# A fused gated recurrence and capacity-limited mixture of experts: where the zero rows are written, how wide, and what keeps TensorE busy around the selection

## The chip, the cores and the metric

The kernel runs on one core of one Trainium2 chip. The metric is device time in microseconds of one execution. Before the change the median of three runs is 306.29 us (305.9 to 307.69).

## The reference

`x`, `r_gate` and `i_gate` have the shape (4, 5056, 256). The first stage is a linear recurrence over time, the second a mixture of 8 experts over its N = 20224 output rows, in which each expert takes at most `capacity` = 80 tokens:

```python
a_t = exp(8 * sigmoid(r_gate) * log(clip(sigmoid(a_param), 1e-6, 1 - 1e-6)))
x_gated = sqrt(max(1 - a_t * a_t, 1e-6)) * sigmoid(i_gate) * x
h = a_t[:, t] * h + x_gated[:, t]; y[:, t] = h              # for every t
logits = y @ w_gate; expert = argmax; gate = softmax(logits)[expert]
out = zeros((N, 256))
for e in range(8):                                          # w1: 256 x 1024, w2: 1024 x 256
    tok = the 80 tokens of expert e with the largest gate
    out[tok] = gate[tok] * (relu(y[tok] @ w1[e]) @ w2[e])
```

At most 640 of the 20224 output rows are not zero.

## The kernel before, in words

**The scan.** The tokens are cut into 40 units of 512 (the last has 256). `Y` is one SBUF buffer of 50 slots, each 128 partitions x 1024 floats; unit u's scan result ends in slot u, and the raw inputs pass through slots that are free at the time. `ORDER` (lines 28 to 50) is the order of all work of this part, written out by hand: a letter and a unit for each task, among them `q` the squares and `p` the gates on POOL (GpSimd), `S` the roots on ScalarE, `U` PE's transposes, `g` and `y` the multiplication and the scan on VectorE, `c` the routing steps, and `Z` one zero fill. PE, ScalarE, VectorE and POOL each run their tasks in this order; every plain DMA is issued from SyncE's queue (SP), in the order of the program.

**The zero fills.** `zero_fill` (line 194) writes the next 256 rows of the output with zeros, 256 KB, from 256 zeroed columns of slot 39, with 1 KB runs. There are 79 of them. `ORDER` has 59; 38 of these come ahead of its task `S38:1`. The other 20 are issued at line 312, behind the loads of the weights of experts 0 and 1 (lines 310 and 311). The weights live in slots 40 to 43 (even experts) and 44 to 47 (odd ones); in each, `w1` comes first and `w2` takes the last two slots.

**The selection** (lines 376 to 449). Each partition's best candidates are ranked with small products and comparisons. `keep_warm(7)` issues seven products of 128x128 by 128x256 to `pd`, which nothing reads. A product on PE (line 440) counts the partitions that might have overflowed into `pfl`; VectorE converts it to the integer `flag` (line 446) behind its two comparisons of line 444. Fourteen products (line 448) give `sel`, which VectorE copies to `chosen`. All five engines load `flag` into a register (line 624) and take one of two branches; here the short one.

**The experts.** In `experts`, two products turn `chosen` into the tokens' columns, which VectorE writes to `col` (line 501); seven more unused products follow. For every expert, `fetch` (line 517) loads 80 columns into registers, in one instruction for each engine: 32 on ScalarE, 24 on POOL, 24 on VectorE. `copies` (lines 523 and 524) then copies each token's values out of `Y`, one small instruction for each token. PE runs `hidden(e)` (the product with w1) and `summed(e)` (with w2) with ScalarE's `relu(e)` between them. `hidden` and `summed` of expert e issue the loads of expert e + 2's weights into the same slots, each as its old weights have been used. Behind `hidden(0)`, ScalarE fetches expert 1's columns and copies half of them before `relu(0)`. The results are scattered to their rows of the output by POOL, which needs the fills landed.

Of the kernel before, what the change touches and what calls it, by code (L numbers as in the profile page):

```python
# [7 lines left out]
F32 = mybir.dt.float32  # L8
# [7 lines left out]
P = 128  # L16
C = 512
EXTRA = 10
ZERO_TOKENS = 256
SHARE = 12  # L20
WARM = (7, 7)
GATHER = (32, 24, 24)
EARLY = 8
TW = 64
# [20 lines left out]
q34 S33:11 y32b i38 l29 U33b x36 p34 g33a l30 r36 g33b l31 y33a r37 e35 y33b U34a p35 Z n36 c3.0 U34b Z g34a n37 Z y34a c3.1 n38 i39 q35 c3.2 U35a Z  # L45
S35:1 g34b Z T36 c3.4 p36 x37 y34b Z T37 Z g35a c3.3 t36 Z c3.5 U35b y35a c3.6 t37 Z r38 e36 g35b U36a c3.7 y35b c3.8 r39 e37 q36 Z c3.9 c3.10 U36b
x38 h0 n39 l32 S36:1 q37 h1 x39 l33 Z h2 l34 Z p37 Z l35 g36a Z S37:1 g36b T38 Z y36a Z T39 y36b Z U37a Z h3 U37b t38 Z g37a Z t39 p38 e38 g37b Z y37a
Z e39 Z y37b q38 U38a S38:1 Z c4.0 U38b Z h4 q39 Z c4.1 c4.2 Z p39 g38a Z g38b S39:1 Z y38a Z y38b Z U39a Z g39a U39b c4.4 Z c4.3 l36 Z y39a l37 g39b
Z l38 c4.5 y39b Z l39 c4.6 Z c4.7 l40 c4.8 Z c4.9 c4.10 Z k0 c5.0 c5.1 Z c5.2 Z c5.3 c5.4 Z c5.5 c5.6 Z c5.7 c5.8 c5.9 Z c5.10
"""  # L50
SLOTS = {
# [7 lines left out]
def moe_kernel(ctx, tc, x, r_gate, i_gate, a_param, w_gate, w1, w2, out, capacity=80):  # L59
    nc = tc.nc  # L60
    B, S, D = x.shape
    N = B * S
# [10 lines left out]
    Y = big.tile([P, NS, 2, C], F32, name="Y")  # L73
    tiny = const.tile([P, 46], F32, name="tiny")
    ident = const.tile([P, P], F32, name="ident")
# [44 lines left out]
    def root(u, ms):  # L120
        for m in ms:
            q = pair('r', u, m)
            nc.scalar.activation(q, q, AF.Sqrt, scale=-0.25, bias=0.25)  # L123
            u += m
        if u == NU: nc.scalar.activation(warm, L[:, :1], AF.Exp)
# [67 lines left out]
    nz = [0]  # L193
    def zero_fill(k):
        for _ in range(k):
            a = nz[0]
            if a >= N: return
            b = min(N, a + ZERO_TOKENS); nz[0] = b; m = (b - a) * D // P // ZC
            nc.sync.dma_start(out[a:b].rearrange("t d -> (t d)").rearrange("(p m c) -> p m c", m=m, c=ZC),  # L199
                              zero.unsqueeze(1).broadcast_to([P, m, ZC]))  # L200
    pl = ps_g.tile([P, 256], F32, name="pl")
    pt = ps_g.tile([P, 512], F32, name="pt")

# [82 lines left out]
    with tc.manual_schedule(engines={E_.Activation, E_.PE, E_.DVE, E_.Pool}):  # L286
        for task in ORDER.split():
            k, v = task[0], task[1:]
            if k in one_of: one_of[k](int(v))
            elif k in some_of: some_of[k](int(v.rstrip('+')), 1 + v.endswith('+'))  # L290
            elif k in half_of: half_of[k](int(v[:-1]), 'ab'.index(v[-1]))
            elif k == 'S': root(int(v.split(':')[0]), [int(m) for m in v.split(':')[1]])
            elif k == 'c': stages[int(v.split('.')[1])](int(v.split('.')[0]))
            elif k == 'Z': zero_fill(1)
    mstack.close()


# [7 lines left out]
    def w1v(e): return wbuf[e % 2][:, :2 * F].rearrange("p (h f) -> p h f", h=2)  # L305
    def w2v(e): return wbuf[e % 2][:, 2 * F:].rearrange("p (c d) -> p c d", d=D)
    FQ = FC // 2
    def load_w1(e, h): nc.sync.dma_start(w1v(e)[:, h], w1[e, h * P:h * P + P])
    def load_w2(e, g): nc.sync.dma_start(w2v(e)[:, g * FQ:(g + 1) * FQ], w2[e, g * F // 2:(g + 1) * F // 2].rearrange("(c p) d -> p c d", p=P))
    for e, g in ((0, 0), (0, 1), (1, 0), (1, 1)): load_w1(e, g)  # L310
    for e, g in ((0, 0), (0, 1), (1, 0), (1, 1)): load_w2(e, g)
    zero_fill(-(-N // ZERO_TOKENS))

    KG, KF = -(-CAP // 8) * 8, 14
    V = 2 * E
# [35 lines left out]
    def keep_warm(n, ps):  # L351
        pd = ps.tile([P, 512], F32, name="pd")
        for _ in range(n): nc.tensor.matmul(pd[:, :256], ident, vvf, start=True, stop=True)  # L353
# [22 lines left out]
    with tc.manual_schedule(engines={E_.Activation, E_.PE, E_.DVE, E_.Pool}):  # L376
# [5 lines left out]
        def lowered(c0, c1):  # L382
            vec.tensor_tensor(vv[:, :, c0:c1], pv[:, :, c0:c1], fm.unsqueeze(2).broadcast_to([P, NR, c1 - c0]), op=ALU.mult)
# [6 lines left out]
        def parts(v, n):  # L390

            for q in range(n):
                src = rest[:, v] if q else vals[:, v]
                pp = src if q == 2 else part[q][:, v]
                if q < 2: pool.tensor_copy(pp, src)
                pool.tensor_tensor(rr[:, :, q, v], pp[:, :K].unsqueeze(2).broadcast_to([P, K, E]),
                                   em.unsqueeze(1).broadcast_to([P, K, E]), op=ALU.mult)
                if q < n - 1: pool.tensor_tensor(rest[:, v], src, pp, op=ALU.subtract)
# [7 lines left out]
        lowered(0, 8); lowered(8, K)  # L406
        keep_warm(WARM[0], ps_t)
        parts(1, 3)
# [5 lines left out]
        wide = lambda v: v.unsqueeze(2).broadcast_to([P, 16, K1])  # L414
# [24 lines left out]
    pfl = ps_t.tile([1, 1], F32, name="pv")  # L439
    nc.tensor.matmul(pfl, fl, one, start=True, stop=True)  # L440
    sel = ps_t.tile([3 * V, CAP], F32, name="sel")
    flag = small[:1, 145:146].bitcast(I32)
    for c0, c1 in ((0, K - 5), (K - 5, K)):
        nc.vector.tensor_tensor(oh[:, c0:c1], rk[:, c0:c1].unsqueeze(2).broadcast_to([P, c1 - c0, CAP]),
                                iot[:, :CAP].unsqueeze(1).broadcast_to([P, c1 - c0, CAP]), op=ALU.is_equal)
        if c0: nc.vector.tensor_copy(flag, pfl)
        for k in range(c0, c1):
            nc.tensor.matmul(sel, rr[:, k].rearrange("p q v e -> p (q v e)"), oh[:, k], start=(k == 0), stop=(k == K - 1))
    nc.vector.tensor_copy(chosen, sel)
# [45 lines left out]
    def experts(own, small_ps, ps):  # L495
# [7 lines left out]
        nc.tensor.matmul(pt, chosen, comb[:3 * V], start=True, stop=True)  # L503
        keep_warm(WARM[1], ps)
        AT = small[:CAP, 96:112]; sidx = small[:CAP, 112:120].bitcast(U32)
# [9 lines left out]
        def fetch(k, e):  # L515
            eng, et, a, b = SPAN[k]
            regs[k] = nc.values_load_multi_w_load_instructions(col[e:e + 1, a:b], engines=[et], min_val=0, max_val=LAST - 1,
                                                               skip_runtime_bounds_check_because="a token's column")[1]
        def copies(k, e, j0=0, j1=64):
            eng, et, a, b = SPAN[k]  # L520
            for j in range(a + j0, min(b, a + j1)):
                src = flat[:, bass.ds(regs[k][j - a], 2, step=C)]; dst = XG[:, e, :, j]
                if k == 'A': eng.copy(dst, src)  # L523
                else: eng.tensor_copy(dst, src)  # L524
# [5 lines left out]
        phs, pos, pys, sent = {}, {}, {}, []  # L530
# [10 lines left out]
        def relu(e):  # L541
            nc.scalar.activation(hbuf[e % 2].rearrange("p (q s) -> p q s", q=2), phs[e][:, :, :FQ * CAP], AF.Relu)  # L542
        def summed(e, only=None):

            h2T = hbuf[e % 2].rearrange("p (c s) -> p c s", c=FC)
            if not only: pos[e] = ps_f.tile([P, 512], F32, name="po", bufs=2)
            po = pos[e]
            def part(c, d):
                for j in QT:
                    nc.tensor.matmul(po[j:j + TW, d * CAP:(d + 1) * CAP], w2v(e)[:, c, d * P + j:d * P + j + TW], h2T[:, c],  # L550
                                     start=(c == 0 and (only is not None or d == 0)), stop=(c == FC - 1 and (only is not None or d == 1)), tile_position=(0, j))
            if only is not None:
                for c in range(FC): part(c, only)
                return
            for c in range(FC):
                for d in range(2): part(c, d)
                if c % FQ == FQ - 1 and e + 2 < E: load_w2(e + 2, c // FQ)
# [29 lines left out]
        ps_f = own.enter_context(tc.tile_pool(name="ps_f", bufs=1, space=bass.MemoryType.PSUM))  # L587
        hidden(0)
        for q in 'APV': fetch(q, 1)
        copies('A', 1, 0, nA // 2); copies('V', 1, 0, nA // 2); copies('P', 1)  # L590
        relu(0)
        copies('A', 1, nA // 2); copies('V', 1, nA // 2)
        for q in 'APV': fetch(q, 2); copies(q, 2)
        rows_of_slots()
        summed(0)
        hidden(1)
        for k in range(1, E):
            e = k + 2 if k + 2 < E else None
# [17 lines left out]
    def arm(before=None):  # L616
        with ExitStack() as own:
            own.enter_context(tc.manual_schedule(engines={E_.Activation, E_.PE, E_.DVE, E_.Pool, E_.SP}))
            small_ps = own.enter_context(ExitStack())
            ps = small_ps.enter_context(tc.tile_pool(name="ps_a", bufs=1, space=bass.MemoryType.PSUM))  # L620
            if before: before(KG, ps)
            experts(own, small_ps, ps)

    _, fv = nc.values_load_multi_w_load_instructions(flag, engines=[E_.PE, E_.DVE, E_.Activation, E_.Pool, E_.SP], min_val=0, max_val=P,
                                                     skip_runtime_bounds_check_because="a count of rows")
# [32 lines left out]
```

## Time and profile before

| | |
|---|---|
| median of three runs | 306.29 us |
| the profiled execution, its own time | 304.79 us |
| its span, first to last instruction | 303.1 us |
| busy share of the span: PE, ScalarE, VectorE, POOL | 76%, 78%, 70%, 69% |
| moved by DMA over the span | 100.91 MB, mean 333 GB/s |

Times in the rows are us from the start of the span, durations of single instructions ns. PE is TensorE (PEld its weight loads), DVE VectorE, ACT ScalarE, SP SyncE; a q behind an engine's name is its sequencer, so SPq rows are SyncE's DMA issues and ACTq rows what ScalarE's sequencer does itself. fp32 products show as two records each. An entry in brackets is the idle time ahead of a group and what ended it. TensorE's granted clock is given as a share of full speed.

### The profile page before, as it was taken

The page shows a single profiled execution, that of the slowest core. Times are in us where ns is not written, and L with a number is a line of the kernel's source. Part 1 is how long each engine was busy: PE and PEld are TensorE (multiplying, and loading weights), DVE is VectorE, ACT ScalarE, POOL GpSimd, SP SyncE. Part 2 cuts the span into 40 slices and gives each one's busy share as a digit, 9 for nine tenths or more (in the row PEclk, how much of TensorE's full clock was granted, in tenths as well). Part 3 has the DMA queues.
Part 4 walks back from the last instruction along what each step waited for, and adds up shares of the span by engine and source line. Part 5 has one row for each costly group of instructions (what it writes and reads, how often), then busy time and mean ns, then how long its engine had stood idle before and what let it go on. Part 6 is the DMA issues. An engine that isn't in the chain of part 4 may idle for free.

```text
span 303.1 us, 8355 instructions
## 1 busy us (share of the span) xinstructions
PE 229.4 (76%) x2764; PEld 187.0 (62%) x2764; DVE 213.1 (70%) x501; ACT 237.1 (78%) x491; POOL 208.5 (69%) x315
## 2 busy tenths in 40 slices
PE   2632798879897898799679897755656957998791
PEld 2522686667667576487477666545534647888681
DVE  1000899799988999698979989999787245465410
ACT  5999999999999998999999999985014138667500
POOL 2477999969789999999548868763035256666512
PEclk9995899999999999979959999997857577999997
DMA  7999899799988999679998999999999995999741
GB/s 217 408 411 408 296 413 407 293 347 343 386 293 280 374 376 410 263 243 365 298 346 310 390 403 371 388 381 367 327 331 371 379 344 209 336 384 384 282 153 32
DMA packets 50499, 100.91 MB, mean 333 GB/s; under 512 B 4368, under 2 KB 32912, under 8 KB 50448
## 3 DMA queue, kind: packets, MB, share of 16 engines
q1 hardware_dynamic: 50064, 99.64, 90.6%
q0 software_dynamic: 384, 0.66, 0.7%
q8 instruction: 24, 0.39, 0.5%
q14 instruction: 27, 0.22, 0.2%
HBM read 78.91 MB, written 21.36 MB: 331 GB/s over the span
## 4 chain that ended last, share of the span: by engine, by line
ACT 19%; DMA 18%; issue 16%; DVE 15%; PE 13%; POOL 8%; SPq 7%; POOLq 2%; ACTq 0%; DVEq 0%
DMA Y<-in_r_gate_dram 7%; DVE Y L151 7%; SPq L199 6%; POOL Y L524 6%; DMA Y<-in_x_dram 5%; PE pu L139 5%; DVE pu L143 5%; ACT Y L128 5%; ACT Y L123 4%; ACT Y L107 4%; ACT Y L116 3%; DMA out_dram<-Y 3%; PE pl L211 2%; DMA Y<-in_i_gate_dram 2%; PE pd L353 2%
## 5 line engine op out<-in xcount | busy, mean ns | idle before, releaser
L139 PE MATMUL pu<-ident,Y 128*128 128x128 f32 x632 | 90.9, 292 | 30.9 <-issue 10.0
L139 PEld LDWEIGHTS pu<-ident,Y 128*128 128x128 f32 x632 | 75.0, 150 | 48.2 <-issue 22.5
L151 DVE TENSOR_TENSOR_SCAN Y<-Y,pu 128x512 f32<-128x512 f32 (+4 forms) x86 | 100.6, 1181 | 3.1 <-DVE pu L143 0.5
L132 POOL TENSOR_TENSOR Y<-Y 128x1024 f32<-128x1024 f32 (+2 forms) x31 | 92.0, 2978 | 11.4 <-DVE Y L151 4.1
L119 POOL TENSOR_TENSOR Y<-Y 128x1024 f32<-128x1024 f32 (+2 forms) x31 | 72.9, 2362 | 23.0 <-ACT Y L116 16.0
L143 DVE SCALAR_TENSOR_TENSOR pu<-Y,pu 128x512 f32<-128x512 f32 (+1 forms) x80 | 53.4, 673 | 34.2 <-PE pu L139 28.4
L105 PE MATMUL pr<-ident,Y 128*128 128x128 f32 x316 | 43.7, 288 | 15.5 <-DMA Y<-in_r_gate_dram 8.3
L116 ACT ACTIVATE Y<-Y,tiny 128x512 f32<-128x512 f32 (+2 forms) x62 | 53.6, 927 | 1.7 <-PE pu L139 1.3
L105 PEld LDWEIGHTS pr<-ident,Y 128*128 128x128 f32 x316 | 37.7, 149 | 19.3 <-ACT Y L107 10.0
L523 ACT COPY Y<-Y 128x2 f32 x256 | 25.5, 190 | 24.8 <-issue 20.3
L128 ACT ACTIVATE Y<-Y 128x1024 f32<-128x1024 f32 (+2 forms) x31 | 38.9, 1284 | 1.8 <-DMA Y<-in_i_gate_dram 1.7
L107 ACT ACTIVATE Y<-pr 128x1024 f32<-128x1024 f32 (+1 forms) x40 | 38.4, 1002 | 1.5 <-PE pr L105 1.4
L211 PE MATMUL pl<-Y 128*32 128x128 f32 (+2 forms) x704 | 39.5, 369 | 0.0
L123 ACT ACTIVATE Y<-Y 128x1024 f32<-128x1024 f32 (+2 forms) x32 | 38.2, 1249 | 0.3 <-POOL Y L119 0.2
L524 POOL COPY Y<-Y 128x2 f32 x192 | 24.3, 202 | 16.3 <-issue 14.7
L524 DVE COPY Y<-Y 128x2 f32 x192 | 21.6, 178 | 19.5 <-issue 19.5
L211 PEld LDWEIGHTS pl<-Y 128*32 128x32 f32 x704 | 20.6, 120 | 11.0 <-issue 4.6
L537 PE MATMUL ph<-Y 128*64 128x80 f32 x512 | 21.7, 243 | 6.9 <-ACT Y L523 4.0
L537 PEld LDWEIGHTS ph<-Y 128*64 128x64 f32 x512 | 20.3, 145 | 8.4 <-issue 8.4
L550 PE MATMUL po<-rows,Y 128*64 128x80 f32 x512 | 21.3, 245 | 3.3 <-ACT rows L542 2.7
L550 PEld LDWEIGHTS po<-rows,Y 128*64 128x64 f32 x512 | 19.8, 146 | 5.0 <-ACT rows L542 2.9
L573 POOL DMA_INDIRECT out_dram<-Y,lg x7 | 6.6, 945 | 13.2 <-DVE Y L570 13.2
(130 smaller groups left out, 152.9 us busy)
## 6 DMA issues: line engine op xcount, KB each, us to landing
out_dram<-Y SPq DMA_DIRECT2D x79, 256.0 KB, 5.2
Y<-in_r_gate_dram SPq DMA_DIRECT2D x39, 512.0 KB, 5.7
Y<-in_i_gate_dram SPq DMA_DIRECT2D x39, 512.0 KB, 6.3
Y<-in_x_dram SPq DMA_DIRECT2D x39, 512.0 KB, 6.5
Y<-in_moe_w_dram SPq DMA_DIRECT2D x32, 512.0 KB, 6.8
Y<-in_i_gate_dram SPq DMA_DIRECT2D x1, 256.0 KB, 6.3
Y<-in_r_gate_dram SPq DMA_DIRECT2D x1, 256.0 KB, 6.2
Y<-in_x_dram SPq DMA_DIRECT2D x1, 256.0 KB, 6.4
```

What stands on the lines that cost most here:

```text
L105: nc.tensor.transpose(pr[:, h, b:nb * P:nb], block('r', u, b, h), ident)
L107: nc.scalar.activation(rslot(u), prs.pop(u)[:, :, :ntok(u)], AF.Tanh, scale=0.5)
L116: nc.scalar.activation(a[:, :, h], z[:, :, h], AF.Exp, scale=L[:, h:h + 1], bias=L[:, h:h + 1])
L119: nc.gpsimd.tensor_tensor(pair('r', u, m), a, a, op=ALU.mult)
L123: nc.scalar.activation(q, q, AF.Sqrt, scale=-0.25, bias=0.25)
L128: nc.scalar.activation(i, i, AF.Tanh, scale=0.5)
L132: nc.gpsimd.tensor_tensor(i, i, v, op=ALU.mult)
L139: nc.tensor.matmul(pu[:, b:nb * P:nb], block(k, u, b, h), ident, is_transpose=True, start=(k == 'x' and b == 0), stop=(k == 'i' and b == n ...
L143: nc.vector.scalar_tensor_tensor(pu, rslot(u)[:, h], 0.5e-3, pu, op0=ALU.max, op1=ALU.mult)
L151: nc.vector.tensor_tensor_scan(y[:, s0:s1], a[:, s0:s1], q[:, s0:s1], init, op0=ALU.mult, op1=ALU.add)
L211: nc.tensor.matmul(pl[32 * j:32 * j + 32, c0:c0 + n], wg[:, h, 24 - E * k:WG - E * k], Y[:, us[0]:us[-1] + 1, h, 4 * j + k:ntok(us[0]):NR] ...
L524: else: eng.tensor_copy(dst, src)
```

## The change

- `ORDER` from `S38:1` on: the engines' tasks stay in their order. A task `W` (POOL zeroes all 1024 columns of slot 47) is put behind unit 38's square, 2 single fills stay, and 10 wide fills `V` stand in for 19 single ones. A wide fill writes 512 rows, 512 KB, from slot 47, with one 4 KB run for each partition.
- Behind `ORDER`, the rest of the output is zeroed ahead of the weights, with wide fills (nine, and one single fill). The weights' loads are ordered by expert, w1 before w2.
- `flag` is converted by ScalarE, ahead of both comparisons of line 444.
- 12 and 11 unused products in place of 7 and 7, and five of 128x128 by 128x128 ahead of `summed(0)`, in the PSUM tile that `summed(0)` then starts.

```diff
-WARM = (7, 7)
+WARM = (12, 11)
+ZSLOT = 47
...
+S38:1 W Z c4.0 U38b Z h4 q39 V c4.1 c4.2 p39 g38a V g38b S39:1 y38a V y38b U39a V g39a U39b c4.4 c4.3 l36 V y39a l37 g39b l38
+c4.5 y39b V l39 c4.6 c4.7 l40 c4.8 V c4.9 c4.10 k0 c5.0 c5.1 V c5.2 c5.3 c5.4 V c5.5 c5.6 c5.7 c5.8 c5.9 V c5.10
...
+    wide = Y[:, ZSLOT].rearrange("p h t -> p (h t)")
+    WIDE = P * 2 * C // D
+    def blank(): nc.gpsimd.memset(wide, 0.0)
+    def wide_fill():
+        a = nz[0]
+        if a + WIDE > N: return zero_fill(-(-WIDE // ZERO_TOKENS))
+        nz[0] = a + WIDE
+        nc.sync.dma_start(out[a:a + WIDE].rearrange("(p b) d -> p (b d)", p=P), wide)
...
-    for e, g in ((0, 0), (0, 1), (1, 0), (1, 1)): load_w1(e, g)
-    for e, g in ((0, 0), (0, 1), (1, 0), (1, 1)): load_w2(e, g)
-    zero_fill(-(-N // ZERO_TOKENS))
+    while nz[0] < N: wide_fill()
+    for e in range(2):
+        for g in range(2): load_w1(e, g)
+        for g in range(2): load_w2(e, g)
...
-        if c0: nc.vector.tensor_copy(flag, pfl)
+        if not c0: nc.scalar.copy(flag, pfl)
...
-            if not only: pos[e] = ps_f.tile([P, 512], F32, name="po", bufs=2)
+            if e and not only: pos[e] = ps_f.tile([P, 512], F32, name="po", bufs=2)
...
         relu(0)
+        pos[0] = ps_f.tile([P, 512], F32, name="po", bufs=2)
+        for _ in range(5): nc.tensor.matmul(pos[0][:, :P], ident, ident, start=True, stop=True)
```

## Rows read from the trace of the kernel before

**Rows 1.** The chain of waits: start us, us, what.

```profile
235.65 6.10 PE pd L353 x14
```

**Rows 2.** Instructions of line 517, 233 to 243 us: count, ns min/median/max, starts.

```profile
L517 ACTq TENSOR_LOAD <-lg x1: 5683/5683/5683, 235.7 to 235.7; - x1
...
L517 DVEq TENSOR_LOAD <-lg x1: 4800/4800/4800, 235.8 to 235.8; - x1
```

**Rows 3.** Line 517, 243 to 250 us.

```profile
L517 ACTq TENSOR_LOAD <-lg x1: 4570/4570/4570, 244.8 to 244.8; - x1
```

**Rows 4.** Line 517, 250 to 255 and 262 to 267 us.

```profile
L517 ACTq TENSOR_LOAD <-lg x1: 1947/1947/1947, 252.4 to 252.4; - x1
...
L517 ACTq TENSOR_LOAD <-lg x1: 2397/2397/2397, 263.1 to 263.1; - x1
```

**Rows 5.** Stretches: engines' busy us, granted clock, DMA share, GB/s.

```profile
206.60:249.30 42.70, 27.40 (x264) 20.95 (x262) 27.57 (x113) 10.83 (x62) 13.62 (x68) 0.71 1.04 356
...
226.00:228.50 2.50, 2.50 (x7) 2.00 (x6) 2.38 (x8) 1.82 (x8) 1.55 (x5) 0.50 1.02 405
236.00:247.00 11.00, 7.62 (x42) 6.04 (x43) 2.81 (x24) 3.23 (x32) 3.06 (x24) 0.66 1.09 381
...
265.00:281.00 16.00, 14.43 (x360) 13.09 (x355) 9.70 (x78) 11.26 (x99) 10.37 (x65) 1.00 1.06 384
```

**Rows 6.** SyncE's time line: start us, us, line, operation, tiles, count.

```profile
194.18 27.25 SPq L199 DMA_DIRECT2D out_dram<-Y  x34
...
229.10 18.27 SPq L199 DMA_DIRECT2D out_dram<-Y  x20
```

**Rows 7.** ScalarE's time line, 234 to 259 us.

```profile
241.63 0.77 ACT L523 COPY Y<-Y 128x2 f32 x7 [10.26 <-issue]
242.56 2.46 ACT L523 COPY Y<-Y 128x2 f32 x25 [0.17 <-issue]
249.48 1.61 ACT L523 COPY Y<-Y 128x2 f32 x16 [4.46 <-PE ph L537]
250.99 0.69 ACT L542 ACTIVATE rows<-ph 128x640 f32<-128x640 f32 x1
...
258.02 0.70 ACT L542 ACTIVATE rows<-ph 128x640 f32<-128x640 f32 x1
```

**Rows 8.** PE's time line, products only, 218 to 256 us.

```profile
224.99 6.33 PE L353 MATMUL pd<-Y,ident 128*128 128x256 f32 x14 [0.55 <-DVE Y L383]
...
232.92 0.77 PE L448 MATMUL sel<-Y 128*48 128x80 bf16 x14 [0.86 <-POOL Y L396]
...
235.58 6.15 PE L353 MATMUL pd<-Y,ident 128*128 128x256 f32 x14
...
245.12 3.92 PE L537 MATMUL ph<-Y 128*64 128x80 f32 x64 [3.38 <-ACT Y L523]
251.74 4.02 PE L550 MATMUL po<-rows,Y 128*64 128x80 f32 x64 [2.70 <-ACT rows L542]
```

**Rows 9.** POOL's groups by shape: count, busy us, mean ns, idle before.

```profile
masks.py:197 POOL MEMSET ident<- 128x128 f32 x1 | 0.2, 205 | 0.3 <-POOLq L644 0.3
```

**Rows 10.** VectorE's time line: the scans of unit 37.

```profile
203.08 2.45 DVE L151 TENSOR_TENSOR_SCAN Y<-Y,pu 128x512 f32<-128x512 f32 x2
```

**Rows 11.** POOL's time line: squares of units 38 and 39, gate of 39.

```profile
203.41 2.89 POOL L119 TENSOR_TENSOR Y<-Y 128x1024 f32<-128x1024 f32 x2 [1.62 <-DMA out_dram<-Y]
206.26 1.28 POOL L132 TENSOR_TENSOR Y<-Y 128x512 f32<-128x512 f32 x1
```

**Rows 12.** PE's time line: the transposes of unit 39.

```profile
211.02 2.30 PE L139 MATMUL pu<-ident,Y 128*128 128x128 f32 x8 [3.14 <-issue]
```

**Rows 13.** Stretches, PE alone: busy us, granted clock, DMA share, GB/s.

```profile
231.00:232.00 1.00, 0.45 (x3) 0.91 1.10 351
```

**Rows 14.** Line 624, the loads of the flag.

```profile
L624 DVEq TENSOR_LOAD <-lg x1: 1069/1069/1069, 233.9 to 233.9; - x1
```

**Rows 15.** VectorE's time line: the columns' write.

```profile
235.39 0.23 DVE L501 TENSOR_SCALAR lg<-pv 8x80 int32<-8x80 f32 x1 [1.36 <-PE pv L498]
```

More of the change, by code (lines that the diff above doesn't have):

```diff
@@ L47 @@
 x38 h0 n39 l32 S36:1 q37 h1 x39 l33 Z h2 l34 Z p37 Z l35 g36a Z S37:1 g36b T38 Z y36a Z T39 y36b Z U37a Z h3 U37b t38 Z g37a Z t39 p38 e38 g37b Z y37a
-Z e39 Z y37b q38 U38a S38:1 Z c4.0 U38b Z h4 q39 Z c4.1 c4.2 Z p39 g38a Z g38b S39:1 Z y38a Z y38b Z U39a Z g39a U39b c4.4 Z c4.3 l36 Z y39a l37 g39b
-Z l38 c4.5 y39b Z l39 c4.6 Z c4.7 l40 c4.8 Z c4.9 c4.10 Z k0 c5.0 c5.1 Z c5.2 Z c5.3 c5.4 Z c5.5 c5.6 Z c5.7 c5.8 c5.9 Z c5.10
+Z e39 Z y37b q38 U38a S38:1 W Z c4.0 U38b Z h4 q39 V c4.1 c4.2 p39 g38a V g38b S39:1 y38a V y38b U39a V g39a U39b c4.4 c4.3 l36 V y39a l37 g39b l38
+c4.5 y39b V l39 c4.6 c4.7 l40 c4.8 V c4.9 c4.10 k0 c5.0 c5.1 V c5.2 c5.3 c5.4 V c5.5 c5.6 c5.7 c5.8 c5.9 V c5.10
 """
@@ L294, in moe_kernel @@
             elif k == 'Z': zero_fill(1)
+            elif k == 'W': blank()
+            elif k == 'V': wide_fill()
     mstack.close()
```

## The prediction, made before the changed kernel was run

> **What bounds the kernel now.** Read the chain of waits first. From 235.65 us it shows 6.10 us under the warming products of L353 [rows 1], and nothing computes from them: the token copies of ScalarE and VectorE that follow wait for their own register loads. So I read L517, the line that loads an expert's token columns into an engine's registers. The first expert's load takes ScalarE 5683 ns for 32 columns and VectorE 4800 ns for 24 [rows 2]; the second expert's takes ScalarE 4570 ns [rows 3]; the later ones take 1947 to 2397 ns [rows 4]. These are single instructions that do the same work each time, so no other engine's lateness is in them.
>
> What differs is what the DMA engines move meanwhile. From 236 to 247 us, at a DMA share of 1.09 and 381 GB/s, they write zeros out of SBUF; from 265 to 281 us, at 1.06 and 384 GB/s, they bring weights into SBUF [rows 5]. The load is slow beside zero fills and fast beside an equal stream of weights. SyncE's queue says why the fills are there: 34 fills, then the eight weight loads of experts 0 and 1, then 20 more fills issued from 229.10 to 247.37 us [rows 6], right over both slow loads. The bound of this stage is a load's round trip beside fills, on ScalarE, which has the most columns.
>
> Then ScalarE's time line [rows 7]: load, 32 copies until 245.02, 4.46 us idle for the second load, 16 copies, relu(0) at 250.99, and on without slack to relu(1) at 258.02. PE's products wait for ScalarE: 251.74 us for summed(0) is the end of that ReLU [rows 8]. So ScalarE's two slow loads stand on the path, one behind the other.
>
> **The change, part by part.**
>
> *Order of fills.* Of the 34 fills behind the last input load, 15 stay, 20 fills become 10 wide ones, and what is left (19 of 79) becomes nine wide fills and one small, all ahead of the weights. By bytes: from 206.6 to 249.3 us the queue moved 42.7 us x 356 GB/s = 15.2 MB [rows 5]. The same 15.2 MB now end with 4.2 MB of weights, so the fills end when 11.0 MB are through. At the fills' present 381 GB/s that is 28.9 us, at 235.5 us; at the 405 GB/s that the 4 KB weight packets reach [rows 5], 27.2 us, at 233.8; at the mean of 356, 30.9 us, at 237.5. I take 235.5: nothing shows a 4 KB write, and 381 is the nearest row of a write. The first load starts at 235.7 now. It runs beside weights then, and so does the second.
>
> ScalarE's loads cost 1.95 to 2.40 us beside weights; I take 2.2. First load: 5.68 - 2.2 = 3.5 us. Second: the idle is the load less 0.1 us of overlap, so 4.46 becomes 2.1, 2.4 us. Together -5.9 us (-5.5 to -6.4 with the two ends; if the fills last to 237.5, about 0.8 us less, because 7 of 32 columns are then read at the slow 5683/32 = 178 ns).
>
> *Weights later.* w1 of expert 0 are the first 1.05 MB behind the fills: 2.8 us, moved by 238.3. hidden(0) wants them when ScalarE's copies end, 236.3 + 2.2 + 3.4 = about 242. The last half of w2 of expert 1 goes to slot 47, so its issue waits for every wide fill to land; it is the last DMA on SyncE before the branch, and summed(1), its reader, comes 10 us later. SyncE itself reaches its branch before its first release by PE instead of at 247.4. Cost nothing; without this cover, a late w1 would delay hidden(0) one for one.
>
> *The blank slot.* The memset of 128x1024 on POOL: 128 columns take 205 ns [rows 9], so at most 8 x 0.205 = 1.6 us, at least 0.2. It waits for the scan of unit 37, which ends at 205.53 [rows 10]. It stands between the two squares of units 38 and 39 [rows 11]; the first, twice as long, ends about 205.3. So the second square and the last gate, now done at 207.54, slip by at most 1.9 us, to 209.5. Who waits: PE's transposes of unit 39, which start at 211.02 after 3.14 us idle [rows 12], and ScalarE's root of unit 39, which VectorE multiplies with their result. Nothing moves. The first wide fill waits for the memset too; fills queued before it still drain then. Cost 0 (0 to 0.5).
>
> *Twelve products, then eleven.* The first set runs from 224.99 at 6.33/14 = 0.45 us per record, two records a product, at the low clock [rows 8]; the clock is granted in full within 231 to 232 us (0.91 in that stretch) [rows 13], about when the seven products end. The five added ones are 10 records at 0.226 us at the full level: 2.3 us, to 233.5. Behind them on PE stand the flag's product (0.19 us) and the 14 selection products, which started at 232.92. They end at about 234.45 instead of 233.69: +0.76 us. Bounds: +0.2 if the clock rises three microseconds earlier, +3.1 if it never rises.
>
> Moving the flag to ScalarE takes a small VectorE copy away, and the copy (0.11 us on ScalarE, [rows 7]) comes as soon as the flag's product ends. VectorE's flag load takes 1069 ns from 233.9 [rows 14], behind its copy of the selection. So the column write L501 [rows 15] can follow the selection 0.2 us sooner than it does now. Net of both: +0.6 us.
>
> The second set starts at 236.2. At the full clock 22 records are 4.8 us and end at 241.0, ahead of hidden(0) at 242; at the low clock 9.7 us, 245.9, which would hold hidden(0). PE is busy nearly throughout up to 234.5 now, so I expect the full level.
>
> *Five products before summed(0).* 10 records of half the width, 1.1 to 2.3 us, in PE's 2.70 us of idle [rows 8]. At the full level summed(0) takes 2.4 us, not 4.02, but relu(1) is held by ScalarE's copies. Worth 0.1, counted as 0.
>
> Sum: -5.9 + 0.6 = -5.3 us. The profiled execution took 304.79 us (span 303.1, 1.7 around it), so 299.5; it lies 1.5 us under the median of 306.29, against which changes are told. Predicted: 306.29 - 5.3 = **301.0 us**, its own range 299.2 to 302.9: a gain of 4.1 (5.5 - 0.8 - 0.6) to 6.4 (the products made up by the flag), and 0.7 us each way for the runs' spread.
>
> **Rivals.**
>
> *The loads stay slow.* Then only the +0.6 remains: 306.9. For it: two slow loads in one run, both soon behind the branch. Against: the second starts ten microseconds behind it and is still at 4570 ns, while the third, at 1947, comes as the fills have ended. The Trainium skill, SBUF — State Buffer, section "SBUF: two separate sides", says that engine ports and DMA ports cannot contend with each other; by that rule the loads would cost the same beside anything and the change would give this 306.9. The two stretches of equal DMA share disagree with it for this kind of load. Chance 0.10.
>
> *The fills are not done in time.* If 4 KB writes run slower, at about 300 GB/s, 11.0 MB last 36.7 us, to 243.3. The first load stays slow, and w1 is moved at 246: hidden(0) starts at 246 to 247, while the second load is fast. The gain is 2.4 less 0.6 less about a microsecond of waiting: 305.5. For it: no 4 KB store is in the trace. Against: loads of 4 KB go faster than those of 1 KB. Chance 0.10.
>
> *PE's queue is the new wait (slower).* If the clock stays low through both sets, the 24 records of the first end at 224.99 + 10.85 = 235.84 and the selection starts at 236.05, +3.1 us; the second set then runs from 238.7 to 248.4, and hidden(0) behind it ends at 252.3 instead of 249.04. Five products at the low clock (2.3 us) bring summed(0) to 254.9 instead of 251.74: 306.29 + 3.2 = 309.5, with the shorter loads hidden behind PE. It decides once no rise comes before 235 us. For it: the clock is low at the start of both sets now [rows 8, 13]. Against: it rose after 6 us of products, both times. Chance 0.10.
>
> **How the numbers follow.** Forecast 0.70; rivals 0.10 each. A difference under 1%, 3.1 us, cannot be told from none. Faster by over 1%: the forecast, 0.70. Within 1%: the first two rivals, 0.20. Slower: 0.10. The range is 299.2 to 306.0: it holds the forecast and the late fills, and leaves out the slow loads' 306.9 and PE's 309.5.
>
> **What would show it.** Right: ScalarE's first two L517 loads at 1.9 to 2.4 us; the last fill issued before the first weight; relu(0) 5 us sooner against the column write. Wrong: a load above 4 us with no fill in flight (the first rival); 1 KB-like or lower GB/s in 212 to 236 us (the second); selection products behind L353 by over 2 us (the third).

## The result, and the profile after

The changed kernel is faster: the median of four runs is 298.9 us, against 306.4. The ratio, 0.965 [0.956, 0.974], is that of the two fast runs alone (294.5 and 297.3 us), since the other two (300.5 and 300.6) lie over 1.5% above the fastest. A second comparison with more runs (e1 below) gave 298.99 against 306.61, ratio 0.974 [0.970, 0.978], which is 8.1 us [6.7, 9.4]; this is the gain that is explained below. Forecast were 5.3 us and 301.0.

The scan stage up to unit 37's second scan, which the change does not touch, takes a different time in every profiled run: that scan ends at 205.53 us before [rows 10] and at 208.95 in the run shown here. So times are compared from that scan's end. VectorE's time line, after (start us, us):

```profile
206.51 2.44 DVE L152 TENSOR_TENSOR_SCAN Y<-Y,pu 128x512 f32<-128x512 f32 x2
...
237.55 0.23 DVE L461 COPY lg<-sel 48x80 f32<-48x80 f32 x1 [1.08 <-PE sel L460]
238.50 0.23 DVE L513 TENSOR_SCALAR lg<-pv 8x80 int32<-8x80 f32 x1 [0.72 <-PE sel L515]
```

The column loads, after, over the whole run (line 517 has become 529):

```profile
L529 ACTq TENSOR_LOAD <-lg x8: 1963/1973/2322, 238.8 to 275.6; - x8
...
L529 DVEq TENSOR_LOAD <-lg x8: 1599/1610/1931, 238.8 to 278.5; - x8
```

None of the eight is slow any more; the first was 5683 ns [rows 2], the second 4570 [rows 3]. SyncE's time line, after, shows why: the wide fills are issued by 233 us and the weights follow. The last fill, issued at 233.0, landed 5.7 us later, at 238.7, just before ScalarE's first load at 238.8.

```profile
197.75 12.52 SPq L200 DMA_DIRECT2D out_dram<-Y  x15
210.38 22.57 SPq L209 DMA_DIRECT2D out_dram<-Y  x19
233.00 1.23 SPq L200 DMA_DIRECT2D out_dram<-Y  x1
234.34 2.41 SPq L319 DMA_DIRECT2D Y<-in_moe_w_dram  x2
```

ScalarE's time line, after, which answers to [rows 7]:

```profile
241.01 0.76 ACT L535 COPY Y<-Y 128x2 f32 x7 [5.04 <-issue]
241.94 2.46 ACT L535 COPY Y<-Y 128x2 f32 x25 [0.17 <-issue]
246.26 1.62 ACT L535 COPY Y<-Y 128x2 f32 x16 [1.86 <-issue]
247.79 0.70 ACT L554 ACTIVATE rows<-ph 128x640 f32<-128x640 f32 x1
...
254.66 0.69 ACT L554 ACTIVATE rows<-ph 128x640 f32<-128x640 f32 x1
```

The wait of 4.46 us for the second load is 1.86. Counted from the end of unit 37's scan:

| us behind that scan | before | after | difference |
|---|---|---|---|
| ScalarE's first column load starts | 30.2 | 29.9 | -0.3 |
| relu(0) | 45.5 | 38.8 | -6.6 |
| relu(1) | 52.5 | 45.7 | -6.8 |
| end of the span | 97.6 | 89.9 | -7.7 |

Nearly all of it is won between the first load and relu(0): 5.68 - 1.97 = 3.7 us at the first load and 4.57 - 1.97 = 2.6 at the second. What follows relu(1) took 45.1 us before and 44.1 here, but 45.4 in e1's run of the same kernel, so that this difference cannot be put down to the change.

PE's time line, after, which answers to [rows 8]:

```profile
228.47 7.20 PE L365 MATMUL pd<-Y,ident 128*128 128x256 f32 x24 [0.55 <-DVE Y L395]
235.59 0.19 PE L452 MATMUL pv<-Y,lg 128*1 128x1 f32 x2
236.76 0.68 PE L460 MATMUL sel<-Y 128*48 128x80 bf16 x14 [0.98 <-POOL Y L408]
...
238.40 6.70 PE L365 MATMUL pd<-Y,ident 128*128 128x256 f32 x22
245.32 2.44 PE L549 MATMUL ph<-Y 128*64 128x80 f32 x64 [0.21 <-issue]
247.68 1.38 PE L605 MATMUL po<-ident 128*128 128x128 f32 x10
248.99 2.43 PE L562 MATMUL po<-rows,Y 128*64 128x80 f32 x64
```

hidden(0) and summed(0) take 2.4 us instead of 3.9 and 4.0; e3, e7 and e12 below have the same with seven and seven products. Here the second set of products does stand ahead of hidden(0): ScalarE's copies end at 244.40 and hidden(0) starts at 245.32. PE's granted clock had fallen to 0.50 of full between 239.4 and 241.4 us, behind a selection in which PE was busy for 0.75 of 2 us, so the 22 records took 6.70 us (5.02 in e1's run). It costs relu(0) nothing: ScalarE copies for expert 1 until about 247.8, and hidden(0) ends at 247.76.

### The profile page after: what moved, and what is told of

Same layout as the page of the kernel before. It is cut to its first block, busy times and chain, and to the rows that moved or that the text cites. A ratio compares the mean times of both kernels' runs of the same rounds, so it can differ in the third digit from the quotient of the medians.

```text
span 298.8 us, 8394 instructions
## 1 busy us (share of the span) xinstructions
PE 229.4 (77%) x2792; PEld 187.9 (63%) x2792; DVE 212.5 (71%) x500; ACT 237.7 (80%) x492; POOL 210.1 (70%) x316
## 5 line engine op out<-in xcount | busy, mean ns | idle before, releaser
L140 PEld LDWEIGHTS pu<-ident,Y 128*128 128x128 f32 x632 | 74.0, 148 | 49.2 <-issue 22.4
L106 PE MATMUL pr<-ident,Y 128*128 128x128 f32 x316 | 46.0, 298 | 16.7 <-DMA Y<-in_r_gate_dram 9.4
L106 PEld LDWEIGHTS pr<-ident,Y 128*128 128x128 f32 x316 | 39.7, 155 | 20.6 <-issue 9.7
L108 ACT ACTIVATE Y<-pr 128x1024 f32<-128x1024 f32 (+1 forms) x40 | 38.5, 1001 | 2.7 <-PE pr L106 2.6
L124 ACT ACTIVATE Y<-Y 128x1024 f32<-128x1024 f32 (+2 forms) x32 | 38.2, 1249 | 1.1 <-POOL Y L120 0.9
L562 PE MATMUL po<-rows,Y 128*64 128x80 f32 x512 | 20.5, 235 | 3.8 <-issue 3.6
L562 PEld LDWEIGHTS po<-rows,Y 128*64 128x64 f32 x512 | 18.7, 137 | 5.9 <-issue 5.3
L549 PE MATMUL ph<-Y 128*64 128x80 f32 x512 | 19.4, 233 | 1.5 <-issue 1.4
L549 PEld LDWEIGHTS ph<-Y 128*64 128x64 f32 x512 | 18.5, 137 | 2.1 <-issue 2.1
```

Source lines behind the costliest of these rows:

```text
L106: nc.tensor.transpose(pr[:, h, b:nb * P:nb], block('r', u, b, h), ident)
L140: nc.tensor.matmul(pu[:, b:nb * P:nb], block(k, u, b, h), ident, is_transpose=True, start=(k == 'x' and b == 0), stop=(k == 'i' and b == n ...
```

## The experiments

**e1: the change once more.**

> The changed kernel again, for the size of its gain and for where it lies. Theory A (all of it is in the tail, where the trace shows 7.7 us between the end of unit 37's scan and the end of the span): ratio 0.97 to 0.98, 7 to 9 us, and in the profile the stretch from the end of unit 37's scan to the end is 89 to 91 us, whenever that scan ends. Theory B (the change also shortens the scan stage): that scan ends 2 us or more before 205.5 us, and the ratio is 0.965 or lower.

Ratio 0.974 [0.970, 0.978]. Unit 37's scan ended at 208.50 us, later than before's, and the tail took 91.2 us instead of 97.6, a little more than the 89 to 91 expected: theory A. The part up to that scan is not shortened; among the runs of this study that scan ends anywhere from 205.5 to 209 us.

**e2: the order alone.** The kernel before, with 1 KB fills, but all of them ahead of the weights:

```diff
+    zero_fill(-(-N // ZERO_TOKENS))
+    for e in range(2):
+        for g in range(2): load_w1(e, g)
+        for g in range(2): load_w2(e, g)
-    ...
-    zero_fill(-(-N // ZERO_TOKENS))
```

> The kernel before with one part alone: the 20 fills of 1 KB runs behind ORDER are issued ahead of the weights. Theory A (a register load is slow beside fills that read SBUF, and nothing else matters much): both first loads of ScalarE at 2.0 to 2.5 us instead of 5.7 and 4.6, relu(0) 5.5 to 6 us earlier against the column write; 299.5 to 301, about 6 us of the gain. Rival B (the first two loads are slow because they come soon after the branch): loads stay at 5.7 and 4.6, 306.4. Rival C (wide fills are needed for the fills to be done): the first load at 3.5 us or more, the second fast, 302.5 to 304.

301.97 us, ratio 0.984 [0.980, 0.988]: 4.8 us. The time lies between the ranges of theory A and rival C. ScalarE's first load took 3562 ns and the second 1981:

```profile
L518 ACTq TENSOR_LOAD <-lg x2: 1981/2772/3562, 239.4 to 246.3; - x2
```

That is rival C on the first load: the 1 KB fills are still in flight when it starts at 239.4 us, the last of them issued at 238.7. Order gives the larger part. relu(0) lies 3.0 us later behind the scan than in the changed kernel: 1.6 is the longer first load, which wide fills, done sooner, avoid; 1.0 is that load's later start, and 0.3 a wait for hidden(0), which took 3.69 us. How the last two divide between width, flag and products this run does not show.

**e3: loads in place of the fills.** The kernel before with 20 loads of the same size and run length in place of the 20 fills, behind expert 0's weights:

```diff
-    zero_fill(-(-N // ZERO_TOKENS))
+    for k in range(20):
+        nc.sync.dma_start(Y[:, NU + 4 + k % 8 // 2, k % 2].rearrange("p (m d) -> p m d", m=2),
+                          xf[k * 256:(k + 1) * 256].rearrange("(m p) d -> p m d", p=P))
```

> The kernel before, with the 20 fills that follow the weights replaced by 20 loads of 256 KB with 1 KB runs into slots 44 to 47, ahead of expert 1's weights; those 5 MB of zeros are left out of the output. The DMA engines stay as busy as before during both first loads. Theory A (it is DMA reads of SBUF that slow a register load): 1.9 to 2.5 us for both, 300 to 302. Rival B (near the branch) and rival D (any full DMA stream): 4.5 us or more for both, 306 to 307.

The loads of columns, and the DMA over the first of them and the copies behind it (the last two numbers are DMA share and GB/s):

```profile
L521 ACTq TENSOR_LOAD <-lg x3: 1968/1975/1975, 237.9 to 248.3; - x3
...
237.00:245.00 8.00, 6.74 (x58) 5.48 (x60) 4.01 (x33) 3.23 (x32) 4.01 (x32) 0.79 1.10 349
```

The DMA engines are full, the loads of columns stand at the same place in the program, and each of ScalarE's takes 1.97 us: B and D fall. relu(0) comes 38.7 us behind the scan, as in the changed kernel. The time, 303.41 (ratio 0.991 [0.987, 0.995]), gains only 2.7 us because expert 1's weights now come behind the 20 loads: relu(1) is at 48.5 instead of 45.7. I had not counted that.

**e8: the wide fills behind the weights.** The changed kernel, with the last half of expert 1's w2 behind them, since it takes their slot:

```diff
-    while nz[0] < N: wide_fill()
     for e in range(2):
         for g in range(2): load_w1(e, g)
-        for g in range(2): load_w2(e, g)
+        for g in range(2 - e): load_w2(e, g)
+    while nz[0] < N: wide_fill()
+    load_w2(1, 1)
```

> The changed kernel with the nine wide fills and the small one behind the weights again, all but the last half of w2 of expert 1, which follows them. Theory A: 4 KB reads of SBUF slow the register loads as 1 KB reads do: ScalarE's first two at 4 us or more, relu(0) as late as before (45 us behind the end of unit 37's scan), ratio 0.99 to 1.00. Rival G (only the 1 KB reads are harmful): loads under 3 us, ratio 0.975 to 0.98.

```profile
L530 ACTq TENSOR_LOAD <-lg x2: 1960/4136/6313, 238.7 to 248.3; - x2
...
238.00:245.00 7.00, 5.38 (x26) 4.31 (x24) 0.66 (x6) 0.00 (x0) 0.31 (x3) 1.00 1.02 416
```

The first load took 6313 ns beside 4 KB fills, no less than beside 1 KB ones (5683 before, 6469 in e4), and relu(0) came 45.3 us behind the scan: width does not protect a load. The second load, 1960 ns, fell behind the fills' end. Ratio 0.995 [0.991, 0.998]: nearly all of the gain is gone with the order.

**e10 and e11: reads of SBUF or writes to HBM?** A fill does both. e10 copies the zeroed columns from SBUF to SBUF, e11 copies rows of x from HBM to HBM, in the place of the 20 fills:

```diff
+        nc.sync.dma_start(Y[:, NU + 4 + k % 8 // 2, k % 2].rearrange("p (m d) -> p m d", m=2),
+                          zero.unsqueeze(1).broadcast_to([P, 2, ZC]))                     # e10
...
+        nc.sync.dma_start(rows_at(out), rows_at(xf))                                      # e11
```

> The kernel before, the 20 fills behind the weights replaced by 20 copies of the same 256 zeroed columns into slots 44 to 47 (SBUF to SBUF), ahead of expert 1's weights; those rows of the output are left out. Theory A (reads of SBUF by DMA): ScalarE's first load at 4 us or more. Rival H (writes to HBM): both loads at 2.0 to 2.5 us.

> The kernel before, the 20 fills behind the weights replaced by 20 copies of rows of x into the output (HBM to HBM), which leaves other values than zeros in those rows. Theory A: no SBUF is read, so both loads take 2.0 to 2.5 us. Rival H (writes to HBM): 4 us or more.

e10 (the first two loads of ScalarE; then the stretch of the first), and e11 likewise:

```profile
L521 ACTq TENSOR_LOAD <-lg x2: 1950/3563/5176, 236.8 to 245.3; - x2
...
236.00:241.50 5.50, 5.50 (x15) 4.23 (x15) 0.53 (x4) 0.00 (x0) 0.39 (x4) 0.50 1.10 351
```

```profile
L520 ACTq TENSOR_LOAD <-lg x3: 1961/1968/1980, 236.4 to 246.8; - x3
...
236.00:245.00 9.00, 8.70 (x80) 7.05 (x80) 5.18 (x43) 4.37 (x45) 5.52 (x44) 0.68 1.01 371
```

5176 ns beside copies from SBUF to SBUF, 1961 to 1980 beside copies from HBM to HBM, and 1.97 us beside e3's loads from HBM to SBUF: of the four kinds of traffic, only the two that the DMA engines read out of SBUF slow a load. One run each: 303.72 and 302.82 us.

One thing does not fit at first sight. In e10 the next loads are quick, although its copies were not through: the last of them, issued at 241.7 us, landed 5.9 us later, at 247.6. e10's next loads, and that copy:

```profile
L521 POOLq TENSOR_LOAD <-lg x1: 1769/1769/1769, 243.7 to 243.7; - x1
L521 DVEq TENSOR_LOAD <-lg x1: 1601/1601/1601, 244.0 to 244.0; - x1
L521 ACTq TENSOR_LOAD <-lg x1: 1950/1950/1950, 245.3 to 245.3; - x1
...
DMA to landing us min/median/max: 5.9/5.9/5.9
```

The slow stretch begins ahead of the landings too: before, VectorE's load of the flag is slow at 233.9 (1069 ns [rows 14]), while the last weight load, which stands in the queue ahead of all 20 fills, landed at 236.8. In e11, the same kernel up to these fills, that load takes 561 ns. If the DMA engines read SBUF some microseconds ahead of a landing, both follow; no run shows the reads by themselves, so this is not shown. Nor does a run test whether it matters where in SBUF the DMA engines read: all the slow traffic came out of one zeroed slot, 39 or 47.

**e4: the products alone** (12, 11 and five, on the kernel before).

> The kernel before with the products alone: 12, 11 and the five. Theory A: the loads stay at 5.7 and 4.6, the selection ends 0.5 to 0.9 us later, summed(0) runs at the full clock or not without moving relu(1) by more than 0.3 us; 306.5 to 307.5. Rival E (the clock is the gain): summed(0) at 2.4 us instead of 4.0 and relu(1) 1.5 us or more earlier, 303 to 305.

Ratio 0.9995 [0.996, 1.003]. The loads stayed slow (6469 and 3428 ns), summed(0) ran in 2.44 us, and relu(1) came 52.7 us behind the scan, against 52.5: theory A, though the time, 305.73 us, lies under its 306.5 to 307.5. A faster PE is worth nothing here while ScalarE waits for its loads.

**e5: the flag alone.**

> The kernel before with the flag's conversion alone moved to ScalarE. Theory A: PE's and VectorE's own loads of the flag (0.99 and 1.07 us beside fills) are what the column write waits for; with the flag about 0.8 us sooner PE's load overlaps the selection products, VectorE's does not, and the column write comes 0.2 to 0.5 us sooner against the end of unit 37's scan (30.1 us before): ratio 0.998 to 1.000. Rival F (the flag is the whole unexplained part): 1 us or more sooner, ratio 0.997 or lower.

Ratio 0.995 [0.991, 0.999], about 1.5 us by the times, but the tail of its profile is 97.5 us, as before's, and the first load starts 30.6 us behind the scan instead of 30.2, with the clock lower over the selection's products (1.13 us instead of 0.77). Inconclusive as to the time. Behind the selection, VectorE waits 1.10 us for the column write instead of 1.36, which is about the 0.2 us forecast for the flag; but the selection ends 0.7 us later, so the column write comes 30.3 us behind the scan, against 29.9 before.

**e6, e7, e9, e12: fewer products in the changed kernel.** e6 leaves out the five; e7 has 7 and 7; e12 has 7 and 7 without the five; e9 has none.

```diff
-WARM = (12, 11)
+WARM = (7, 7)        # e7, e12; (0, 0) in e9
...
-        for _ in range(5): nc.tensor.matmul(pos[0][:, :P], ident, ident, start=True, stop=True)   # e6, e9, e12
```

> The changed kernel without the five products ahead of summed(0). Theory A: relu(1) is set by ScalarE's copies, so at most 0.2 us: ratio 0.972 to 0.980. Rival E (the clock they keep is worth something): summed(0) falls to the low clock, 4.0 us instead of 2.4, hidden(1) and relu(1) come 1 us or more later, ratio 0.977 to 0.985.

> The changed kernel with 7 and 7 products as before. Theory A: the five added ones of the first set cost 0.3 to 0.8 us ahead of the selection, so without them it ends that much sooner; hidden(0) runs at the low clock (3.9 instead of 2.4 us) and relu(0), held by ScalarE's copies until then, is 0 to 0.5 us later. Ratio 0.970 to 0.980, no difference that can be told. Rival E (the clock is worth something): relu(0) 1 us later and the ratio 0.978 to 0.985.

> The changed kernel with 7 and 7 products and none ahead of summed(0): the best guess at a version that beats both. Theory A: the column write 0.5 to 0.9 us sooner than in the changed kernel, relu(1) at 44.5 to 45.5 us behind unit 37's scan: ratio 0.968 to 0.976. Rival E: summed(0) at the low clock, relu(1) at 46.5 or later, ratio 0.978 to 0.985.

> The changed kernel with no unused product at all (0, 0 and none ahead of summed(0)). Theory A (the order of the fills is the whole gain, the products only stand ahead of the selection): relu(1) at 44.5 to 46 us behind the end of unit 37's scan (45.7 in the changed kernel), though hidden(0) and summed(0) run at the low clock: ratio 0.968 to 0.980. Rival E (the clock is worth something once the loads are short): hidden(0) 3.9 and summed(0) 4.0 us put PE behind ScalarE; relu(1) at 47 or later, ratio 0.980 to 0.988.

| | products | ratio | first load starts | relu(0) | relu(1) |
|---|---|---|---|---|---|
| changed (e1's times, the first run's profile) | 12, 11, 5 | 0.974 [0.970, 0.978] | 29.9 | 38.8 | 45.7 |
| e6 | 12, 11, 0 | 0.970 [0.963, 0.977] | 29.5 | 38.5 | 45.3 |
| e7 | 7, 7, 5 | 0.976 [0.970, 0.982] | 29.0 | 38.0 | 44.8 |
| e12 | 7, 7, 0 | 0.976 [0.971, 0.981] | 29.3 | 38.2 | 45.0 |
| e9 | 0, 0, 0 | 0.981 [0.977, 0.986] | 29.3 | 39.4 | 46.3 |

(The last three columns are us behind unit 37's scan.) The five added products of the first set hold the column load back by 0.9 us (first row against e7) or 0.2 (e6 against e12). The five ahead of summed(0) buy nothing: without them, in e6, it takes 2.43 us all the same. Nor do the added products bring hidden(0) to 2.4 us. I had expected 3.9 us for it in e7, but it took 2.43 there, 2.44 in e12 and 2.43 in e3; in these runs PE stands idle for about 1 us ahead of it. In the runs with slow loads (before, e2, e4, e5, e8, e10) PE stands idle for 2.8 to 5.4 us ahead of it, and it took 3.7 to 4.5 us, with seven products or with eleven.

No products at all costs about 1.2 us of relu(0) against e12, whose first load starts at the same time: PE runs hidden(0) at the low clock (granted 0.50, then 0.57 of full), in 4.39 us, and relu(0) waits for it. e9 and e12 on PE:

```profile
241.53 4.39 PE L549 MATMUL ph<-Y 128*64 128x80 f32 x64 [5.74 <-ACT Y L535]
```

```profile
241.85 2.44 PE L549 MATMUL ph<-Y 128*64 128x80 f32 x64 [1.03 <-ACT Y L535]
```

So rival E is right by about a microsecond, once the loads are short and there are no products at all; e9's relu(1), at 46.3 us, lies between the two ranges. Of e6, e7 and e12 none can be told from the changed kernel by its time; no version beats it.

## Why the prediction was wrong

Its mechanism was right, and the size too small: 5.3 us forecast, 8.1 [6.7, 9.4] measured, and 298.9 lies 0.3 us under the range. (Taken off 306.29, the interval of the gain gives 296.9 to 299.6, so it reaches just into the range.) Of the 2.8 us that are missing, the net of products and flag is 0.9, the loads are 0.4, and the rest, most of it behind relu(1), is open.

- **The loads** were the gain, as forecast, and for the reason given: -6.3 us in the trace against -5.9. I took 2.2 us for a load beside weights; it is 1.97 for nearly all of them.
- **When the fills end.** Forecast 235.5 us, 30.0 behind the scan, at 381 GB/s. The last fill landed 29.7 us behind the scan, as forecast. The wide fills went faster than I took, at 408 GB/s, near the 405 that I had only as the other end:

```profile
213.00:233.00 20.00, 12.13 (x156) 9.38 (x157) 16.59 (x55) 3.94 (x18) 5.23 (x18) 0.74 1.02 408
```

- **The net of products and flag, +0.6 us, was the step that failed.** It came out at -0.3, the first row of the table (-0.1 in e1's profile). The selection products end 28.5 us behind the scan instead of 28.2, +0.3 and not +0.76: the 24 records took 7.20 us, not the 8.6 forecast, because the clock rose sooner in this run (granted 0.98 of full from 232 us; in e1's run 0.90 from 234), and the selection then waited 0.98 us for POOL's line 408 and no longer for the products. (In e1's run they took 8.50, the selection followed at once, and it is +0.5.) And VectorE waits 0.72 us ahead of the column write instead of 1.36, a gain of 0.6 where I allowed 0.2. The reason is the loads of the flag, which I had priced at the old 1069 ns [rows 14]. They are the same kind of instruction, and beside no fills they shorten as the column loads do. After:

```profile
L638 ACTq TENSOR_LOAD <-lg x1: 982/982/982, 236.0 to 236.0; - x1
...
L638 PEldq TENSOR_LOAD <-lg x1: 551/551/551, 236.9 to 236.9; - x1
...
L638 DVEq TENSOR_LOAD <-lg x1: 564/564/564, 237.7 to 237.7; - x1
```

ScalarE, which loads the flag at 236.0 beside the last fills, still needs 982 ns; PE and VectorE, a microsecond later, 551 and 564. Three other runs separate short loads from the moved flag. VectorE's idle time ahead of the column write is 0.87 us in e3, where the flag stays on VectorE and PE's and VectorE's loads of it are short (486 and 562 ns); 1.10 in e5, where the flag is moved and they are slow; and 1.34 in e8, which has the change's flag and products but slow loads of it (1108 and 1187 ns):

```profile
237.58 0.23 DVE L505 TENSOR_SCALAR lg<-pv 8x80 int32<-8x80 f32 x1 [0.87 <-PE pv L502]
...
237.98 0.23 DVE L501 TENSOR_SCALAR lg<-pv 8x80 int32<-8x80 f32 x1 [1.10 <-PE sel L503]
...
238.34 0.23 DVE L514 TENSOR_SCALAR lg<-pv 8x80 int32<-8x80 f32 x1 [1.34 <-PE pv L511]
```

So most of the 0.6 is the short loads. I applied the mechanism to two instructions and missed the third on the same path.

- **The blank slot and the later weights** cost nothing, as forecast: the memset took 0.95 us, between the bounds of 0.2 and 1.6, and w1 of expert 0 landed at 242.4 us, 2.9 ahead of hidden(0).
- **The rest, 1.3 us** between 6.8 us at relu(1) and the 8.1 of the times, lies inside the interval, and the traces do not agree on it (44.1 and 45.4 us behind relu(1) in two runs of the same kernel). It is left open. With the 6.8 alone the time would be 299.5 us, inside the range.
- **The rivals.** That the loads stay slow fell: they take 1.97 us. The Trainium skill, SBUF — State Buffer, section "SBUF: two separate sides", says that engine ports and DMA ports cannot contend with each other. Whichever way a sequencer's loads reach SBUF, the runs show no such freedom for them: beside DMA traffic out of SBUF they took 4.4 to 6.5 us (before, e4, e5, e8, e10). That the fills are late fell (408 GB/s), but e2 shows how near it is with 1 KB runs. That PE's queue becomes the wait is there on a small scale: 0.9 us ahead of hidden(0) in the run shown, at no cost to relu(0).

## What to carry to other kernels

When several engines stand still after a result is ready and the profile says only "issue", look at their sequencers' rows: a register load from SBUF has a duration of its own, and here it was two to three times as long while the DMA engines carried data out of SBUF. Put large stores ahead of the stretch that loads registers, or behind it, and let DMA writes into SBUF run there instead. Then price every such load on the path with the new traffic, the single ones too.

## What the runs showed of the hardware

- A load of 32 registers took 1.97 us beside weights, beside 1 KB loads at 349 GB/s and beside HBM-to-HBM copies at 371, with 2.0 to 2.8 us for some later ones. It took 4.4 to 6.5 us with fills or copies out of SBUF beside it, at 351 to 416 GB/s.
- A single register took 0.47 to 0.57 us in the quiet case (0.67 once, beside e11's copies), and 0.9 to 1.6 beside such fills or copies.
- The slow stretch ran ahead of the landings: loads were quick 1.8 us before the last fill landed in the changed kernel and 3.9 us before the last copy landed in e10.
- Zeros went out at 408 GB/s in 4 KB runs and at 381 in 1 KB runs [rows 5], at DMA shares of 1.02 and 1.09.
